# Sixteen weight loads begun on ScalarE's transfer queue, and the table of instruction orders searched anew

## The chip, the core and the metric

The kernel runs on one core of a Trainium2 chip. The metric is device time in microseconds (us): the median over runs of the time of that core. The core has five instruction streams that run side by side and meet at semaphores: TensorE (PE in the profile), VectorE (DVE), ScalarE (ACT), GpSimd (POOL) and SyncE (SP), which here only begins transfers. Each stream takes its own instructions strictly in order.

## The reference

Clustered attention feeds a block that mixes with a Fourier transform and then applies a feed-forward layer. Sizes: batch 4, 8 heads, 768 tokens, head size 64, so the model width is 512.

```python
def _attn_ref(q, k, v, centroids):
    ...
    q_assign = np.argmax(np.einsum('bhsd,hcd->bhsc', q_n, c_n), axis=-1)
    k_assign = np.argmax(np.einsum('bhsd,hcd->bhsc', k_n, c_n), axis=-1)
    mask = q_assign[:, :, :, None] == k_assign[:, :, None, :]
    scores = np.where(mask, scale * np.matmul(q, k.transpose(0, 1, 3, 2)), -1000000000.0)
    ...
    return np.matmul(attn, v)

def _moe_ref(x, w_ch1, w_ch2):
    u = x + np.real(np.fft.fft(np.fft.fft(x, axis=1), axis=2))
    ...
    return u + np.maximum(un @ w_ch1, 0.0) @ w_ch2
```

`un` is `u` normalized over the width; the weights are 512 x 2048 and 2048 x 512.

## The kernel before

All products are made in pieces of 16 bits: a float32 value is split into a high and a low half (f16), and three products of halves are added in PSUM, the memory that TensorE writes.

**Attention** goes by pairs of heads, 16 pairs in all, four to a sequence. A pair's queries and keys are loaded (L372), scaled and split (L397 on ACT, L398 on DVE), and assigned to clusters. Then 6 row tiles of 128 queries follow (`scores`). A tile's score group for the two heads, j = 0 and 1, is twelve matmuls of L538 and four of L543, which alternate between the two heads' banks `ps_big`. DVE takes the row extremum (L557), which frees the bank early, since in the first sequence it also copies the scores into a ring of four slots in `X[1]`; ACT makes the exponential (L560) and casts it to the high half (L568); POOL subtracts for the low half (L569), which gives back the ring slot; SP begins a transfer that transposes both halves (L571); PE multiplies by V (`attend`, L589 to L591); DVE divides into `X` (L605).

**Weights.** Both weight matrices arrive as 64-bit floats and are loaded as 32 pieces of 128 x 512 (512 KB; in the rows 128 rows of 2048 16-bit words), pieces 0 to 15 of the first layer and 16 to 31 of the second (`Weights.load`, L715). The top bits are split by sign on ACT for two pieces at a time (`signs`, L744 and L745), PE sums them to find the block's largest value (L725) and rebuilds the value (`join`, L754, and L758 on DVE, which reads the raw piece for the last time and so frees its slot); ACT and DVE or POOL make the two halves (`halve`, L764, L767, L768, L770). Pieces 16 to 31 pass through two pairs of slots by turns, so that piece p waits for the join of piece p - 4 (16 and 17 for 4 and 5). A load goes to SP's queue while its number is below `QW`, and to ACT's from there on:

```python
    QW = 99
    ...
        (self.nc.sync if k < self.QW else self.nc.scalar).dma_start(out=raw[:, 1:1 + 4 * DM], in_=src.bitcast(U16))
```

**Fourier and feed-forward.** When the four pairs of a sequence are done, its transform follows (L884 to L1069), then the normalization with transposes (L1106 to L1124), then the feed-forward layer in three blocks (`up`, L1286; `down`, L1314). It runs while the next sequence's attention runs.

**What sets the order.** The program is recorded as Python calls it, and `Order.apply` then sorts each engine's instructions by a table, `ORDERS`, of one compressed row of displacements per engine. It adds dependencies that keep that order and changes nothing that an instruction does. The waits between engines follow from the data.

Of the kernel before, what the change touches and what calls it, by code (L numbers as in the profile page):

```python
# [67 lines left out]
class Counted:  # L68
# [5 lines left out]
    def tile(self, shape, dt, name, bufs=None, **kw):  # L74
# [10 lines left out]
        "QHitW)Rs#sE_5x=9d(_-bbjjHVkdJBA&qWLr8jEKPTWjO9$N*i*IoO1EDrS-OO5|!^uo-vd4T#CtHsVQ??+ZCLUvTEGZIFXYqep@QTV>`l)`pLU$"
        "Za#MPy7k<GpCP}wg%*H`d`0Y9os>DAs#mh=)JQ3=55OzGV7xc-)|LF4qLj7u(%Aw1hjKg@uU@bPaZpPsEA>YDk8RKRg%D?4m8?3c8M2Q^6`3D85A"
        "r{#HPo1>eedDk2IiU)Y0XI98Eg5Ddqs??sM|65y|FXKKi>CZL<j{Wv9>CB!+Y?#v|w|%=2CZDU8z^-Y$fi7{43?{?Br72r7Dy#>{^z*fN_br)`{c"
        "RQ=Ju!`eJ1daV>piss(s1{nmJ8VO^Cxvg*4kd>-RlQDfG5u-Nk!YVth`#hMfat!=ii*o^3oxc&^UZRoKXqHZ3cm4~N1Ie<7b0(bRSw`D10A+<*pb"
        "2$Y9<3!92=%dQ9uj47Ou+Zz=nmwm=sn>GfKSR7f9)^2s3H3koJ4@xODrZV9&)0TNUhi|X*`Jr*FQNH!uAlHf2W0dIae2?2aCF3z7P!#rjpqCm|7t"
# [1499 lines left out]
```

## Time and profile before

| | us |
|---|---|
| median of 3 runs | 954.57 |
| lowest and highest run | 952.27, 954.65 |
| span of the profiled execution | 949.3 |
| PE, DVE, ACT, POOL busy | 863.9, 678.2, 601.6, 608.3 |

The span reaches from the first to the last instruction of one profiled execution; the page gives no other time of that execution, and what lies around the span is in the runs' times. The busy times are sums over the whole span, in which the first quarter and the rest look quite different, so they have to be read by stage. Beginning a transfer is not counted as busy time, on SP and on ACT alike. In rows of the trace, L715 is line 715 of the kernel before; `<-` stands between what an instruction writes and what it reads.

### The profile page before, as it was taken

What the parts mean: (1) busy time and instruction counts of PE and PEld (TensorE: products, weight loads), DVE (VectorE), ACT (ScalarE), POOL (GpSimd) and SP (SyncE); (2) the same over time, 40 slices, a digit from 0 to 9 for tenths busy, and PEclk for the clock granted to TensorE, in tenths of its full rate; (3) what the DMA queues carried; (4) which work ended last, traced back from release to release, by engine and by line L of the source; (5) the groups of instructions that cost most, each with busy time, mean ns of one, the idle gap of its engine ahead of it and who ended that gap; (6) DMA issues with size and microseconds to landing.
All of it is one profiled execution on the core that took longest, in us unless ns stands there. A gap on an engine that the chain in (4) does not pass through costs nothing.

```text
span 949.3 us, 23660 instructions
## 1 busy us (share of the span) xinstructions
PE 863.9 (91%) x9241; PEld 581.0 (61%) x9241; DVE 678.2 (71%) x1531; ACT 601.6 (63%) x944; POOL 608.3 (64%) x752
## 2 busy tenths in 40 slices
PE   4777776677999999998999999999999999999998
PEld 1334443345756748666758667667668586676674
DVE  7989888877756667677757567678773446889643
ACT  6989988776666747647757747657676563353320
POOL 3778786755876876746767768748677764342421
PEclk9999897889999999999999999999999999999999
DMA  9999999988588888999899889998887764201020
GB/s 360 242 217 192 233 262 222 224 169 159 103 169 144 146 178 164 184 177 173 157 171 184 174 155 187 197 173 187 151 147 153 132 118 101 60 1 41 19 78 23
DMA packets 405151, 150.20 MB, mean 158 GB/s; under 512 B 383024, under 2 KB 391728, under 8 KB 405040
## 3 DMA queue, kind: packets, MB, share of 16 engines
q1 hardware_dynamic: 404896, 148.67, 78.1%
q8 instruction: 72, 1.18, 0.5%
q14 instruction: 39, 0.32, 0.1%
q10 hardware_dynamic: 144, 0.03, 0.0%
HBM read 41.99 MB, written 6.29 MB: 51 GB/s over the span
## 4 chain that ended last, share of the span: by engine, by line
PE 56%; DMA 7%; DVE 5%; POOL 4%; ACT 4%; issue 2%; SPq 1%; ACTq 0%; POOLq 0%; DVEq 0%
PE ps_fb L1314 8%; PE ps_fc L1314 7%; DMA pts<-ph 7%; PE ps_fa L1286 6%; PE ps_fa L1314 5%; PE ps_fb L1286 5%; PE ps_fc L1286 5%; PE ps_big L530 5%; PE ps_big L1228 3%; POOL ph L569 2%; PE ps_o L589 2%; PE ps_o L590 2%; PE ps_o L591 2%; PE ps_big L538 1%; ACT ph L568 1%
## 5 line engine op out<-in xcount | busy, mean ns | idle before, releaser
L569 POOL TENSOR_TENSOR ph<-p,ph 128x768 f16<-128x768 f32 x144 | 238.4, 1656 | 112.8 <-ACT ph L568 96.8
L557 DVE TENSOR_SCALAR_CACHE_REDUCE ps_big<-ps_big,sce 128x768 f32<-128x768 f32 x144 | 145.4, 1020 | 60.5 <-PE ps_big L530 34.7
L1314 PEld LDWEIGHTS <-arena 128*128 128x128 f16 x1152 | 109.9, 98 | 121.4 <-issue 1.6
L560 ACT ACTIVATE p<-ps_big,rmx 128x768 f32<-128x768 f32 x144 | 128.7, 897 | 60.3 <-DVE ps_big L557 43.0
L568 ACT CAST ph<-p 128x768 f16<-128x768 f32 x144 | 119.6, 830 | 70.0 <-DMA pts<-ph 67.7
L1295 POOL TENSOR_TENSOR arena<-arena 128x256 f16<-128x256 f32 x160 | 110.8, 697 | 52.2 <-ACT arena L1294 51.6
L1286 PEld LDWEIGHTS <-w1h 128*128 128x128 f16 x1280 | 124.9, 98 | 17.9 <-issue 1.5
L589 PE MATMUL ps_o<-v,pts 128*128 128x66 f16 x1062 | 111.1, 194 | 3.9 <-DMA pts<-ph 2.1
L590 PE MATMUL ps_o<-v,pts 128*128 128x64 f16 x1062 | 110.3, 195 | 0.0
L591 PE MATMUL ps_o<-v,pts 128*128 128x66 f16 x1062 | 110.0, 193 | 0.0
L589 PEld LDWEIGHTS <-pts 128*128 128x128 f16 x1062 | 98.4, 97 | 13.7 <-issue 5.9
L590 PEld LDWEIGHTS <-pts 128*128 128x128 f16 x1062 | 98.4, 97 | 7.4 <-issue 2.6
L1314 PE MATMUL ps_fb<-w2h,arena 128*128 128x512 f16 x320 | 100.9, 379 | 0.0
L591 PEld LDWEIGHTS <-pts 128*128 128x128 f16 x1062 | 98.6, 99 | 0.4
L538 PE MATMUL ps_big<-u 64*128 64x384 f16 x576 | 71.7, 356 | 26.2 <-ACT p L560 13.0
L1286 PE MATMUL ps_fa<-arena,w1h 128*128 128x256 f16 x464 | 85.5, 273 | 0.0
L1314 PE MATMUL ps_fc<-w2h,arena 128*128 128x512 f16 x256 | 81.0, 379 | 0.3 <-ACT arena L1294 0.3
L1286 PE MATMUL ps_fb<-arena,w1h 128*128 128x256 f16 x424 | 78.3, 273 | 0.7 <-DVE arena L1056 0.4
L530 PE MATMUL ps_big<-u 96*128 96x384 f16 (+1 forms) x384 | 75.6, 325 | 2.4 <-ACT p L560 2.3
L1286 PE MATMUL ps_fc<-arena,w1h 128*128 128x256 f16 x392 | 72.4, 273 | 1.1 <-ACT arena L1294 1.1
L1286 PEld LDWEIGHTS <-w1l 128*128 128x128 f16 x640 | 62.5, 98 | 10.6 <-issue 1.6
L538 PEld LDWEIGHTS <-u 64*128 64x128 f16 x576 | 30.1, 100 | 54.3 <-issue 33.9
(371 smaller groups left out, 2149.2 us busy)
## 6 DMA issues: line engine op xcount, KB each, us to landing
arena<-in_moe_w_ch_dram SPq DMA_DIRECT2D x26, 512.0 KB, 5.6
scr<-in_k_dram SPq DMA_DIRECT2D x16, 384.0 KB, 4.3
scr<-in_q_dram SPq DMA_DIRECT2D x16, 384.0 KB, 4.2
vst<-in_v_dram SPq DMA_DIRECT2D x16, 384.0 KB, 4.1
out_dram<-arena SPq DMA_DIRECT2D x24, 256.0 KB, 2.8
u<-u SPq DMA_DIRECT2D x64, 96.0 KB, 2.7
u<-u SPq DMA_DIRECT2D x16, 192.0 KB, 3.2
pts<-ph SPq DMA_TRANSPOSE x161, 3.9
```

Of the source, the lines that this page charges most:

```text
L530: nc.tensor.matmul(out=ps[j][:, hf, 0:SH], lhsT=self.slots(x + 2 * j, 1)[0:n, sl], rhs=self.slots(y + 2 * j, 1)[0:n, hf * SH:(hf + 1) * SH ...
L538: nc.tensor.matmul(out=ps[j][:, hf, 0:SH], lhsT=hq[rows[j], a, sl], rhs=hk[rows[j], c, hs], start=(i == 0), stop=False)
L557: self.mark = nc.vector.tensor_scalar(out=ju, in0=ps[j][:, :, 0:SH], scalar1=ne, scalar2=None, op0=ALU.mult, op1=ALU.min, accum_out=m)
L560: nc.scalar.activation(x, ju, AF.Exp, bias=m, scale=-1.0)
L568: nc.scalar.copy(out=ph[:, 0], in_=p32)
L569: nc.gpsimd.tensor_tensor(out=ph[:, 1], in0=p32, in1=ph[:, 0], op=ALU.subtract)
L589: nc.tensor.matmul(out=o[:, at:at + W], lhsT=hi, rhs=v16[:, kt, 0:W], start=(kt == 0), stop=False)
L590: nc.tensor.matmul(out=o[:, at:at + D], lhsT=hi, rhs=v16[:, kt, 66:130], start=False, stop=False)
L591: nc.tensor.matmul(out=o[:, at:at + W], lhsT=lo, rhs=v16[:, kt, 0:W], start=False, stop=(kt == ST - 1))
L1286: nc.tensor.matmul(out=ps.rearrange("p (t x) -> p t x", x=P), lhsT=a[:, dc, fs], rhs=c[:, :, dc], start=(i == 0), stop=(i == 11))
L1295: nc.gpsimd.tensor_tensor(out=hl[:, f], in0=r, in1=hh[:, f], op=ALU.subtract)
L1314: nc.tensor.matmul(out=ps, lhsT=a[:, f, ts], rhs=w[:, f], start=(i == 0), stop=(i == 47))
```

## The change

`QW` goes from 99 to 16, so that the sixteen pieces of the second weight matrix are begun by ACT and not by SP. All five rows of the table `ORDERS` are new.

```diff
 ORDERS = {
     "Activation": (
-        "c-m!E*>2Q85G;?!dyx?3P=fM+1W16y|9=Hf@CG6h2qXyNNV4o{dz<R&@d9Ek+vAz(?&|95SpcZ8v&47ed(5w`ZLG6n#INSv8j#W8qxts{_td;w`%"
...
+        "c-l=>X>Suj4E4+&X|ARxh@%35_`;9iSMxvkf)JuYNFYQ@ucRSIv)MJzZ@imkmCf#q$M4yGc0@#iG#c?6rPe+CZnVO6#GN1+c5Ag=kw5s&<P^^vp18*QG0*"
...
     AHEAD = 7
-    QW = 99
+    QW = 16
     LOW = 16
```

The table is 19 lines longer, so that every line behind it has a number higher by 19 in the changed file: L715 is L734 there, L538 is L557, L571 is L590, L744 and L745 are L763 and L764, and L764 and L767 are L783 and L786. In the rows below, `in_moe_w_ch2_dram` is the second weight matrix in memory, `ph`, `p32`, `pts` and `u` hold the halves of attention before and after a transpose, `ps_big` is a score bank, and the number behind a name tells one buffer's use from the next.

SP's queue about the last weight loads, from the third row tile of sequence 0's last pair on, before:

```order
L571 DMA_TRANSPOSE u_109<-p32_2136 128x12x128
L472 DMA_TRANSPOSE u_109<-oh_115 128x9x128
L571 DMA_TRANSPOSE pts_110<-ph_2223 128x12x128
L715 DMA arena_67<-in_moe_w_ch2_dram 128x2048 x4
L571 DMA_TRANSPOSE pts_110<-p32_2230 128x12x128
L571 DMA_TRANSPOSE pts_110<-p32_2348 128x12x128
L571 DMA_TRANSPOSE pts_110<-ph_2341 128x12x128
L571 DMA_TRANSPOSE pts_110<-ph_2446 128x12x128
L571 DMA_TRANSPOSE u_109<-p32_2453 128x12x128
L715 DMA arena_67<-in_moe_w_ch2_dram 128x2048 x2
L571 DMA_TRANSPOSE pts_110<-ph_2546 128x12x128
L715 DMA arena_67<-in_moe_w_ch2_dram 128x2048 x2
```

The same place in the change:

```order
L590 DMA_TRANSPOSE pts_110<-ph_2223 128x12x128
L491 DMA_TRANSPOSE u_109<-oh_115 128x9x128
L590 DMA_TRANSPOSE pts_110<-p32_2230 128x12x128
L590 DMA_TRANSPOSE pts_110<-p32_2348 128x12x128
L590 DMA_TRANSPOSE pts_110<-ph_2341 128x12x128
L590 DMA_TRANSPOSE pts_110<-ph_2446 128x12x128
L590 DMA_TRANSPOSE u_109<-p32_2453 128x12x128
L991 DMA arena_67<-in_ny_dram 128x384
L590 DMA_TRANSPOSE pts_110<-ph_2546 128x12x128
L590 DMA_TRANSPOSE pts_110<-ph_2554 128x12x128
L391 DMA scr_2791<-in_q_dram 128x768
```

The eight loads of `in_moe_w_ch2_dram` between the transposes are gone, and a table load of the Fourier stage (`ny`) stands further ahead; the transposes follow each other in nearly the same order.

ACT about the halving of pieces 18 and 19 (`ps_fb_1953` and `ps_fa_2040`), before:

```order
L560 ACTIVATE X1_64<-X1_64,rmx_2021 128x768
L428 ACTIVATE ac_2140<-ps_fc_2141,cinv_176 128x384
L568 CAST ph_2024<-X1_64 128x768
L764 ACTIVATE w2h_82<-ps_fa_2040,wsc_1779 128x512
L764 ACTIVATE w2h_82<-ps_fb_1953,wsc_1779 128x512
L560 ACTIVATE X1_64<-X1_64,rmx_2028 128x768
L560 ACTIVATE X1_64<-X1_64,rmx_2133 128x768
L767 ACTIVATE arena_67<-ps_fa_2040,wsc_1779 128x512
L560 ACTIVATE X1_64<-X1_64,rmx_2126 128x768
L745 ACTIVATE w2l_83<-arena_67 128x1024
L361 ACTIVATE v16_2035<-vst_1301,scp_65 128x6x64
L744 ACTIVATE w2h_82<-arena_67 128x1024
```

The same place in the change:

```order
L783 ACTIVATE w2h_82<-ps_fb_1953,wsc_1779 128x512
L734 DMA arena_67<-in_moe_w_ch2_dram 128x2048
L447 ACTIVATE ac_2140<-ps_fc_2141,cinv_176 128x384
L587 CAST ph_2024<-X1_64 128x768
L734 DMA arena_67<-in_moe_w_ch2_dram 128x2048
L579 ACTIVATE X1_64<-X1_64,rmx_2028 128x768
L763 ACTIVATE w2h_82<-arena_67 128x1024
L783 ACTIVATE w2h_82<-ps_fa_2040,wsc_1779 128x512
L764 ACTIVATE w2l_83<-arena_67 128x1024
L786 ACTIVATE arena_67<-ps_fa_2040,wsc_1779 128x512
L579 ACTIVATE X1_64<-X1_64,rmx_2126 128x768
L763 ACTIVATE w2h_82<-arena_67 128x1024
```

The loads of pieces 22 and 23 now stand between casts and exponentials, and behind them come the sign steps (L763, L764) of pieces 20 and 21 and, in the last row shown, the first one of pieces 22 and 23.

PE at the score group of `ps_big_1173` and `ps_big_1174`, the fifth row tile of the second pair, before:

```order
L590 LDWEIGHTS u_109
L590 MATMUL ps_o_658<-v16_265,u_109 128x64
L591 LDWEIGHTS u_109
L591 MATMUL ps_o_658<-v16_265,u_109 128x66
L538 LDWEIGHTS u_109
L538 MATMUL ps_big_1173<-u_109 128x384
L538 LDWEIGHTS u_109
L538 MATMUL ps_big_1174<-u_109 128x384
L538 LDWEIGHTS u_109
L538 MATMUL ps_big_1173<-u_109 128x384
L538 LDWEIGHTS u_109
L538 MATMUL ps_big_1174<-u_109 128x384
```

In the change the first matmul of that group stands so (the second one, on `ps_big_1174`, comes 28 matmuls of attention times V later):

```order
L562 LDWEIGHTS u_109
L562 MATMUL ps_big_1059<-u_109 128x384
L557 LDWEIGHTS u_109
L557 MATMUL ps_big_1173<-u_109 128x384
L610 LDWEIGHTS pts_110
L610 MATMUL ps_o_658<-v16_219,pts_110 128x66
L608 LDWEIGHTS pts_110
L608 MATMUL ps_o_658<-v16_219,pts_110 128x66
L609 LDWEIGHTS pts_110
L609 MATMUL ps_o_658<-v16_219,pts_110 128x64
```

The sixteen matmuls of a score group stood in a row; now the first one stands ahead, and matmuls of an older tile's `attend` fill the place between it and the others.

## Rows read from the trace of the kernel before

**Rows 1.** The page's part 1, busy time, share and instructions of each engine, whole span.
```profile
PE 863.9 (91%) x9241; PEld 581.0 (61%) x9241; DVE 678.2 (71%) x1531; ACT 601.6 (63%) x944; POOL 608.3 (64%) x752
```

**Rows 2.** Windows by stage; columns PE, PEld, DVE, ACT, POOL busy (x instructions), clock, DMA, GB/s.
```profile
40.00:200.00 160.00, 112.86 (x1431) 61.12 (x1428) 140.66 (x293) 136.29 (x176) 121.92 (x109) 0.88 1.09 224
200.00:240.00 40.00, 33.29 (x441) 24.19 (x439) 29.77 (x80) 27.60 (x45) 24.67 (x30) 0.94 0.81 138
240.00:949.00 709.00, 696.15 (x7215) 485.54 (x7212) 473.06 (x1077) 407.06 (x683) 444.09 (x556) 1.00 0.71 135
```

**Rows 3.** Line L1286 (first feed-forward layer): count, ns min/median/max, first and last start.
```profile
L1286 PE MATMUL ps_fa<-arena,w1h x464: 269/273/274, 232.7 to 850.3; 128*128 128x256 f16 x155
```

**Rows 4.** Waits of DVE, 40 to 200 us: us in total, times, longest.
```profile
DVE ps_big L557 <- PE ps_big L543: 2.6, 3, 1.9
...
DVE X L557 <- PE ps_big L543: 2.3, 4, 1.1
DVE X L557 <- POOL ph L569: 1.8, 2, 1.0
DVE arena L899 <- ACT arena L897: 1.2, 2, 0.7
...
DVE X L557 <- POOL p L569: 0.7, 1, 0.7
```

**Rows 5.** Waits of ACT, same stretch.
```profile
ACT X L560 <- DVE X L557: 6.6, 6, 2.0
...
ACT ph L568 <- DMA pts<-ph: 2.8, 4, 0.8
```

**Rows 6.** Waits of POOL, same stretch.
```profile
POOL ph L569 <- ACT ph L568: 10.8, 10, 3.4
...
POOL p L566 <- DMA u<-p: 1.7, 2, 0.9
```

**Rows 7.** Waits of PE, same stretch.
```profile
PE ps_big L538 <- DVE X L557: 10.3, 11, 1.8
PE ps_big L538 <- ACT p L560: 9.4, 5, 4.2
```

**Rows 8.** Line L715, weight loads begun from 50 to 180 us, and their landing.
```profile
L715 SPq DMA_DIRECT2D arena<-in_moe_w_ch_dram x16: 327/410/889, 56.1 to 175.7; - x16
...
DMA to landing us min/median/max: 3.7/5.3/7.1
```

**Rows 9.** Waits of SP's queue, 40 to 200 us.
```profile
SPq L715 <- DVE ps_fa L758: 5.6, 4, 2.0
```

**Rows 10.** Line L571, transposes that SP began from 40 to 200 us.
```profile
L571 SPq DMA_TRANSPOSE pts<-ph x27: 1273/1543/3362, 41.1 to 194.2; - x27
L571 SPq DMA_TRANSPOSE pts<-p x15: 1274/1755/5428, 38.2 to 159.9; - x15
```

**Rows 11.** Timeline of SP's queue, 150 to 165 us: start, us, line, operation, count.
```profile
152.66 4.36 SPq L715 DMA_DIRECT2D arena<-in_moe_w_ch_dram  x4
157.12 6.00 SPq L571 DMA_TRANSPOSE pts<-p  x2
```

**Rows 12.** Line L1447, ACT's only DMA issue, at the start.
```profile
L1447 ACTq DMA_DIRECT2D X<-in_centroids_dram x1: 403/403/403, 0.7 to 0.7; - x1
```

**Rows 13.** Groups of ACT by line, 40 to 200 us: busy us, mean ns, idle before.
```profile
L560 ACT ACTIVATE X<-X,rmx 128x768 f32<-128x768 f32 x42 | 38.2, 932 | 6.6 <-DVE X L557 6.6
...
L744 ACT ACTIVATE w2h<-arena 128x1024 int16<-128x1024 int16 x8 | 9.7, 1214 | 0.4 <-DMA arena<-in_moe_w_ch_dram 0.4
...
L764 ACT ACTIVATE w2h<-ps_fa,wsc 128x512 f16<-128x512 f32 x8 | 5.5, 682 | 2.2 <-DVE ps_fa L758 1.8 <-DVE wsc L65 0.4
```

**Rows 14.** Timelines of PE from 29 us and from 237.5 us; idle before in brackets.
```profile
29.20 0.32 PE L538 MATMUL ps_big<-u 64*128 64x384 f16 x1 [0.41 <-DVE X L557]
30.13 1.13 PE L538 MATMUL ps_big<-u 64*128 64x384 f16 x11 [0.62 <-DVE X L557]
...
238.05 1.15 PE L538 MATMUL ps_big<-u 64*128 64x384 f16 x12
```

More of the change, by code (lines that the diff above doesn't have):

```diff
@@ L85 @@
[L85 to L89, printed above, removed]
@@ new lines @@
+        "|xm&z>A2q8a&FR?UCfw@O4@x7<6GzvQ&<T<*ML$+BQn_sm4_eD0zQ9s1h28;`>CQi1mmR4<*WslCwo7OEzfg{EgyN+wA)wibwOaZjPgj7TLFY|&e+l`CYW"
+        "Nm0f#QfUQIrkXN6a2?LI?a)2v{Xl!u)c^<^D$weddk@>0An(W|$``V?I3lZ*_^&njI)H*x{Cn(;wO2abtq&8PVYO>pHFX-R67_m3mpFIcovRUFf%QAx<;?"
+        "14U0b5(#TAj%H1wFJnyO^?zI*yd=3``Pr`$erDXzk;_ud0kUh9hb>v<L0tAthQ)k+>xoeSzac3Mtzz^YNxk4=Ic8J}y(sbDk7=10zGOye8IX^LMuV&NDoP"
+        "4PwPbvkQRHs~f(0lQboUDB9!{(G|Mqhgs?s%2aOWu+;bXY$K4ThPl=chL&#l@Tv#A-LXK4d>`Dn-NFyP1`IQLgStqVjpw5AD{w9a>0|an~Hr}2k55OGz&}"
@@ new lines @@
+        "T>QA$C;WI&+n2<h-MNy0#7Gq3CPt%#NvKE`Pvx!%XC2JW^IWvCHMH<7FIIba0pIPU(ZYw8gk9I^tZOic7>MoxP!B6`jq=JLO^~Uz1)(%f%0UrQ}lRE_<Gn"
+        "r&By)hCy#LGAdLZucfJCttRD%_+q|xNj~L$jSr<KWunxK^Bb$O9Pd)qk`r+z?p{X|xj&cIAe^!Cog$ZXE)$z5KZ0tm<Zpu+y|xFv=U1$OIh~7gt2U^PTCq"
+        "#LnAmt<c$Y<G?tp&n;+-WoMpRx9)w}YD7`Ie7RBe{b{3}I8>8e$qu5m?N@7Y=v?+$q0JsUL{-u89&7|!FIGbPV(#@l#n&a{wUzULV`VanJ`^>M2I<i*SqW"
+        "+^{{x;rXU$@PYAzPIN>^E@UsrD`cC4)?c2V2yNCc6S#g*IPN7iHAE>F{(DN#tVbG(t9K8&-@=Pq5IB-rTa3d!~OY9J-F6Q7W=nX)7{PCS@XMP#D5j<xINu"
@@ L110 @@
+        "fW9uqg=cY+3KDMf1wR)kvQ;i?ot7!<0dtvTuZ&h<e>!WfmTbeSpG>xM_Y@Xr986<qfSK2$*uK7I&XWII1ty??yioIFojHAEcXMVt^;;yV{CB>Gie$U`eJy"
+        "!OUGL8SClppw8GfB%{ef2cYywd$#`7N%!o9vTQG5B8gjk{~A)q<IOW??<gichmXra5q;*bRd-JMcapXk3=^e{wdBE3=|$GAVig#>~AN9V>f1;u}vecU7K="
+        "@^6YhF?uGBp0)88)WH{o"
     ),
     "DVE": (
[L112 to L113 removed]
@@ new lines @@
+        "Guk`GacyN`R9Yc${kZqY7>RK{G7<-LdRtKR3SU7dYp-p8oV6$<DtZc>U-c9rn7%|uoFCip!|pRlKI3>|Ql8W`>ItRnE}Bz+A}=hWt(Ot}ZS628l);b99aB"
+        "7KwaO#a@ZSE$3A*t5-bJhyelKX_iDpSVCpJm2Rztn0!5lXQ<|kB4YU(O1=qtlwo{BiiE$2eg3EA!h4%XW(6~Pw8#Gfw>A9hkJrOVsTl$cHm(dEDo`w1kVr"
+        "fyNB;0Mq_T%JK*Y)GWsj-J#Z{YQttB}uc!q<Fye@IV6#d4uxAt}n`ko9rvlawxuJLj@zb=9d}Vwk$lw<C&ciRkE752C94#T2f_4Ge#)!_)7|h6Z2fn&2Q4"
+        "_EcFrUtOA99iIVr>i2muL-~2nzw7G0*Z<j$uzw9&>t-drVp8QpENmRz!4#Z$TM0Z^GA@g>xCno^?d9g5Qv2J_H8Q;e?ITiJ@CSSHpP8p|Wr6iglofNpMw^"
@@ new lines @@
+        "$0OCmK;Nc6*eax?%*@j@^%>ACoiMY!2FnuB8EAI_>s$EVK$JZe#wUot$0u+q6Yb6b<pw`b->Z^CyqjPobyOx{BGJ4j*tx?;RT4pe_xOS`>^W-{D1L*5^)c"
+        "IASVn#aim|FzavhPdpK=GNJXEIeaGwR$GX2J7MKuK4o~vZ}6ydv}qdtd}Re0cd`Oteam8^xzq4*fXwhz5*v8{8<@nwDqERA3x#Bahk`2=hfXj8Rg6rJ5`p"
+        "wfn$D*_|AOw0X!^VY<wO)w|Wn)M)d12FI|UsMhQwRWK13iMEI)iIy&s@l4VJnwR*OR3sz9%=6&60Qz7WiLl>uYyLH;fe6vq;JeqT16>$`6#o-RbB*~_PMM"
+        "(Qa*&;N1DlmJ=O3jjGBtlLv@K-BKXf3i7~FDvwh5=a-L}C@aP4)u4<AVRYdfbA76DJz|R03ppJaSy2e(#L@-A`v-HLhqV2KZ-A9LArEj4G-&qjcP4u-d!E"
@@ new lines @@
+        "UHbTMHHJn$htc*zLJWu+<<@i3VaYH_e;aT7-|TcBf;|mhJF1{x-US)Y^zix%dJKd`3Og5O<UQ=7;FB;-SO-RR6X*7WGSKGm4z@?k(@n(+?~?L#nQ*_DS!d"
+        "_N+_%GTC~Q_tK>Vh2*6G%K`8nS1a4t-_Oqu+wTvZN=C4oYUc}Gt@*0ER4dZ5P;$C`13gpDnjtv%r=l=)9JRHC8nyjEs(8W^J>4E@?-{ttssmYDd-)Eyzph"
+        "BjTK%EZP9Jr?<~od=GBI|YrQ52tDwr(5mQPvzKG5DIx-DqUc}_p#Z3Ufv1JSjx!^Rw-f-1<zZPaC=8LN_LV;@{>D#D4&dWwAQLU~5d64~eH9m8m*hU{zh`"
+        "dXWE4O|`CJY7S4=UuL25|vin$>cqj>Cn}g?F}7t6O*3^W!MZ{CktF}_aCceqqAwA4U_A&re{!~9mPgul_H%c2I>H(^Ht5wMO28dwmqDg4f;xJ_jURJ@y{a"
@@ L151 @@
+        ">&EKTF%Ar#z`H%6f&2EKtHKz%Mw{K3cE~aSIwB`G2?SdB2XwTQ@olx}DsaoeJ5%owaap`(Y?D;;k=-*<MrD_{8Wo156J8^<Uo#p=ngOfc6?wrlNwQr*BIV"
+        "A%<Jdv#b*M>~;kHeN3?Q2jXXb-~TO~PWS`90zBfxDndOcGY;n=2tW86DSmDkyD8L+r^Y=_=DVQ^y<(cyKQEkcV$=Rvk@*;K0<!(YJ_vndneM{F$Ot_dzq-"
+        "_6d-g+o2i4OivE)>gSlxu=>t&+O_JOZmK9Bao&m3=fjHsGmG%b$@YGhZLYEurz$(^srIvoW9+Ty&fi7sIK7qsKN~vt{{R}Uj?w"
     ),
```

110 lines of the change are left out of this document (54 added, 56 removed).

## The prediction, made before the changed kernel was run

> **What bounds the kernel now.** I read the page first, then windows by stage, then the waits of each engine inside the stage that came out. The page gives PE 91% busy [rows 1]. The windows show that this is a mean over two different stages. From 240 us to the end PE is busy 696.15 of 709 us with the full clock granted, so that stage is as long as its matmuls; from 40 to 200 us PE is busy only 112.86 of 160 us, while DVE is busy 140.66 and ACT 136.29, and the DMA engines' share is 1.09 [rows 2]. The feed-forward's first matmul starts at 232.7 us [rows 3]; after that little can be won, so what counts is when it starts. In the early stage DVE is the fullest engine. It waits there for PE's score matmuls (2.6 and 2.3 us) and for POOL's subtractions, which give back the ring slots it writes (1.8 and 0.7 us); for ACT it waits longest 1.2 us [rows 4]. ACT waits 6.6 us for DVE and 2.8 us for transposes [rows 5]; POOL waits 10.8 us for ACT and 1.7 us for a transpose [rows 6]; PE waits 10.3 us for DVE and 9.4 us for ACT before a score group [rows 7]. So four engines and SP's queue lean on each other, all nearly full, with DVE first.
>
> The profiled span is 949.3 us. The runs shown have a median of 954.57 us, 5.27 us above it; I make the sum against the span and add 5.27 us.
>
> **The change, part by part.**
>
> *SP loses 16 loads.* Each issue took 0.41 us there (median; 0.327 to 0.889) [rows 8]: 16 x 0.41 = 6.6 us. SP also stood 5.6 us in front of these loads until DVE's join had freed the slot [rows 9], with transposes queued behind. That is 12.2 us of 160 us that SP gets back. A third effect goes the same way: four loads began at 152.66 us, and the two transposes behind them took 6.00 us, about 3 us each, where the median is 1.54 to 1.76 us [rows 10, 11]. What of it lies on the path is what others lose to late transposes: ACT 2.8, POOL 1.7, and DVE 1.8 + 0.7 = 2.5 us through POOL's ring slots, at most 7.0 us in all [rows 4 to 6]; at least nothing, since DVE itself never waits for a DMA in that stage. I take 4.0 us: ACT's 2.8 and half of DVE's 2.5. What is late next is POOL, which waits for ACT's casts.
>
> The bytes do not change, and the DMA share is already 1.09 [rows 2], so the transfers themselves still compete. The Trainium skill's page "DMA: Bandwidth & Descriptors", section "Issuing engines are not separate DMA queues", says that a second issuing engine saves only the time that the sequencer needs to begin the transfer. By that rule the 3 us transposes would stay as they are, and I would take 2 us instead of 4 us and come to 952.6 us.
>
> *ACT gains 16 issues.* They stand in ACT's order between the casts and exponentials. No row shows ACT issuing in this stage; its only issue, at the start, took 0.40 us [rows 12], and SP's row has the same 0.41 us, so 16 x 0.41 = 6.6 us, at most 16 x 0.889 = 14.2 us if it passes whole, and at least nothing if it falls into ACT's waits (6.6 + 2.8 us in the two rows shown) [rows 5, 8]. The slot waits do not come along in full: nearly every load stands next to the first halving of a piece that needs the same join, so ACT would wait there anyway. POOL, PE and then SP queue behind ACT, but DVE, the fullest, waits for it little. I take a bit under a third of 6.6 us, +2.0 us.
>
> *Landing.* Between the issue of piece 23 and ACT's first reader of it stand two exponentials (0.93 each), two sign steps (1.21 each) and two 512-wide ops (0.68 each): 1.86 + 2.42 + 1.36 = 5.6 us [rows 13]. Landing took 5.3 us at the median, 7.1 us at most [rows 8]. Pieces 19 and 27 have about the same lead, so the cost is 0 to 3 x 1.5 = 4.5 us; by the median nothing, and I take 0.
>
> *PE's order, searched anew.* The set of 1958 matmuls that stand ahead of the first feed-forward matmul is the same in both, but they are cut finer. Before, a score group's first matmul ran alone, and PE then stood 0.62 us until the second bank was free, with nothing put in between [rows 14]. Now the first matmul goes ahead, attention-times-V matmuls follow, and then the rest: the score matmuls stand in 110 separate runs instead of 38 before the feed-forward. A score matmul that runs alone takes 0.32 us, one in a run of twelve 1.15 / 12 = 0.10 us [rows 14], so 72 more runs cost PE up to 72 x 0.22 = 16 us. The cover is PE's idle time, 160 - 112.86 = 47 us [rows 2]; without it, DVE would wait for score banks by that much. On the gain side stand DVE's two waits for score matmuls, 4.9 us [rows 4], since a filled wait lets the older tiles finish earlier. Range -4.9 to +16 us; I take -2.0 us, nearer to the gain because the cover is three times the cost.
>
> *The rest of the new order.* The last write of sequence 0's attention output is DVE's instruction 292 in both orders, and the last split of its first Fourier stage moves from 336 to 339. Three DVE instructions of at most 1 us are 3 us, so -3 to +3 us; I take 0. After 240 us PE is idle 709 - 696.15 = 12.9 us [rows 2], and I count nothing there.
>
> Sum: -4.0 + 2.0 + 0 - 2.0 + 0 = -4.0 us, a span of 945.3 us and a time of **950.6 us**. A measurement of this kernel can tell about 0.3%, 2.9 us, from no change, so this counts as faster, though not by much.
>
> **The rivals.**
>
> *No change (954.6 us).* DVE's own queue is the bound: it is busy 140.66 of 160 us, and no row shows it waiting for SP [rows 2, 4]. Then what SP gets back only lengthens SP's waits, and the two other terms cancel: 0 + 2.0 - 2.0 = 0. For it speaks that DVE's share stays as it was in both orders; against it the 2.5 us that DVE loses to POOL's ring slots.
>
> *Slower: ACT held at the descriptor generator.* If only one queue at a time can have descriptors made, each load on ACT waits until SP's transpose in progress is through, and a whole chain of casts and exponentials stands behind it. By their medians the two kinds of transposes shown held SP for 27 x 1.54 + 15 x 1.76 = 68 of 160 us [rows 10], and with the long ones and the other kinds well over half of the time. Half of a median transpose is 0.8 us; as an upper price every load pays it: 16 x (0.41 + 0.8) = 19 us on ACT. Half of it passes, since POOL and PE already wait for ACT more than for anything else: +9.7 us instead of +2.0. SP's gain is halved to -2.0, because SP meets ACT's loads there too. -2.0 + 9.7 - 2.0 = +5.7 us, 960.3 us. It decides when the mean issue on ACT exceeds about 0.75 us, where a half of 16 x 0.75 equals the 6 us of gain. For it: on SP a load right behind a transpose took up to 0.889 us against 0.327 us [rows 8]. Against it: those were on one queue, and the median is 0.41 us.
>
> This is a rule of the Trainium skill as well: its page "Perfetto Trace Analysis", section "DMA Instruction — HWDGE (DVE, Sync)", says that the block that makes descriptors is locked for exclusive use, and that the wait for the lock lies inside the duration shown. What the trace has of two queues at once is only the start, where ACT's issue took 0.40 us [rows 12].
>
> *Slower: the cut score groups.* If the fill between the first and second score matmul is longer than the wait it hides, score banks come late and DVE, which has little left to do meanwhile, waits. Half of the 16 us passing instead of -2.0 gives 950.6 + 10 = 960.6 us.
>
> **How the numbers follow.** Faster as summed, 0.43; no change, 0.32; the generator, 0.18; the cut groups, 0.07. Hence faster 0.43, same 0.32, slower 0.25. The low end takes SP's whole 7.0 us and 4 us from PE's order with nothing lost on ACT, -11 us, 943.6 us, and a little for the rest of the order: 942.5 us. The high end takes in the two slower cases up to 960 us. The likeliest case alone reaches from 945 to 952 us.
>
> **What would show it.** Right: ACT's loads with a median near 0.41 us; transposes behind no load longer than 2 us; ACT's waits for transposes and DVE's for POOL's subtractions smaller between 40 and 200 us; the first feed-forward matmul at about 229 us instead of 232.7 us; the stage after it as long as before. The generator: load issues on ACT of 1 us and more, and POOL's wait for casts above 10.8 us. The cut groups: DVE's waits for score matmuls above the 4.9 us of its two rows, with PE busier and the first feed-forward matmul later. The whole reading is wrong if the difference arises after 240 us, where I count nothing.

## The result, and the profile after

The changed kernel took 962.73 us (median of 4 runs, 961.53 to 971.17); the kernel before, on the same chip, 954.61 us (4 runs, 952.27 to 956.18). The recorded ratio, taken over all the runs, is 1.0121, 95% interval 1.0083 to 1.0158: slower by 1.2%. By the medians it is 8.1 us, 0.85%. I had forecast 950.6 us, a gain of 0.4%, and had given 960.0 us as the upper end. The profiled execution, the one of 961.53 us, has a span of 959.5 us, 10.2 us more than that of before. In every run of which both are known the time is 1.7 to 2.2 us above the span, so the profile of before (949.3 us) belongs to a time of about 951.2 us, below all four timed runs: some 2 us of the 10.2 us are that profile's luck. Of the 5.27 us that I added to the span, too, only about 2 us lie around a span; this changes neither the gain forecast nor the time. One execution of e14 below (963.49 us) ran in a slower state of the chip and is left out.

The page's part 1 [rows 1 before]:

```profile
PE 887.2 (92%) x9241; PEld 589.0 (61%) x9241; DVE 681.4 (71%) x1531; ACT 603.3 (63%) x944; POOL 614.6 (64%) x752
```

The same three windows of after, with the columns of [rows 2]:

```profile
40.00:200.00 160.00, 126.89 (x1440) 67.15 (x1439) 133.79 (x295) 134.30 (x175) 122.66 (x113) 0.85 1.11 221
200.00:240.00 40.00, 36.50 (x463) 26.16 (x461) 34.87 (x84) 27.88 (x46) 24.81 (x26) 0.95 0.94 167
240.00:949.00 709.00, 693.43 (x7171) 483.17 (x7169) 477.49 (x1070) 410.47 (x685) 450.49 (x558) 1.00 0.70 134
```

and line L1305, which is L1286 of before [rows 3]; every line of after stands 19 further down:

```profile
L1305 PE MATMUL ps_fb<-arena,w1h x424: 269/273/418, 232.6 to 853.4; 128*128 128x256 f16 x142
```

The first feed-forward matmul starts at 232.6 us, as before (232.7). In the early stage PE is busier (126.89 us for about as many matmuls: more of them run alone, and the granted clock, a mean of TensorE's two levels of 1.2 and 2.4 GHz, is 0.85 where it was 0.88) and DVE less (133.79 against 140.66). So in these two profiles the first stage as a whole is neither shorter nor longer, and the 10.2 us arise behind it, where I had counted nothing.

The early stage has changed inside, though. The loads begun on ACT from 40 to 240 us, to be held against [rows 8]:

```profile
L734 ACTq DMA_DIRECT2D arena<-in_moe_w_ch_dram x16: 334/334/1014, 46.2 to 179.1; - x16
...
DMA to landing us min/median/max: 3.9/5.2/11.0
```

An issue on ACT is short (0.334 us at the median). The median landing is as before (5.2 against 5.3 us), but the longest is 11.0 us where it was 7.1. Waits from 40 to 200 us: of ACT [rows 5],

```profile
ACT ph L587 <- DMA pts<-ph: 9.1, 3, 6.6
ACT w2h L763 <- DMA arena<-in_moe_w_ch_dram: 6.1, 2, 5.5
```

of POOL [rows 6],

```profile
POOL ph L588 <- ACT ph L587: 18.4, 11, 3.4
```

and of DVE [rows 4]:

```profile
DVE w2l L789 <- ACT w2h L783: 6.5, 2, 5.3
...
DVE X L576 <- PE ps_big L562: 4.2, 6, 1.3
...
DVE ps_big L576 <- PE ps_big L562: 1.1, 1, 1.1
```

ACT waits 9.1 us for transposes instead of 2.8, once for 6.6 us, and 6.1 us for landed pieces, where [rows 13] had 0.4 us. DVE in turn waits 5.3 us once for ACT's half of a piece. Its waits for POOL's subtractions fell, as I had said, from 2.5 to 0.3 us. The rows don't tell why these transfers came late; that took the experiments.

Behind 240 us, PE's waits in after, to the end:

```profile
PE ps_big L549 <- DMA u<-u: 4.0, 4, 1.5
PE ps_fb L1010 <- DMA u<-u: 3.0, 1, 3.0
PE ps_big L549 <- ACT arena L1074: 1.8, 1, 1.8
```

These are L530, L991 and L1055 of before. Summed over the rows of the matmuls, the gaps between one matmul's end and the next one's start come to 15.6 us behind the first feed-forward matmul; before they were 9.2 us. The other 3.9 us are time in matmuls: in two 20 us windows of after the granted clock is 0.91, a mean of the two levels that costs some 0.09 x 20 = 1.8 us in each, with PE idle in or just ahead of them. Before, the clock stayed at 1.00, the upper level.

```profile
580.00:600.00 20.00, 18.18 (x234) 14.57 (x232) 11.71 (x26) 14.01 (x24) 14.96 (x15) 0.91 0.81 175
...
640.00:660.00 20.00, 18.64 (x218) 14.45 (x219) 13.54 (x29) 13.76 (x21) 11.05 (x12) 0.91 0.78 134
```

### The profile page after: what moved, and what is told of

Read it like the earlier page. It is cut to its first block, busy times and chain, and to the rows that moved or that the text cites. A ratio compares the mean times of both kernels' runs of the same rounds, so it can differ in the third digit from the quotient of the medians.

```text
span 959.5 us, 23667 instructions
## 1 busy us (share of the span) xinstructions
PE 887.2 (92%) x9241; PEld 589.0 (61%) x9241; DVE 681.4 (71%) x1531; ACT 603.3 (63%) x944; POOL 614.6 (64%) x752
## 4 chain that ended last, share of the span: by engine, by line
PE 44%; DMA 18%; ACT 11%; DVE 10%; POOL 9%; issue 5%; SPq 2%; ACTq 0%; POOLq 0%; DVEq 0%
DMA pts<-ph 13%; PE ps_fb L1333 6%; POOL ph L588 5%; PE ps_fc L1333 5%; PE ps_fa L1333 4%; PE ps_fa L1305 4%; PE ps_fc L1305 3%; PE ps_big L549 3%; PE ps_fb L1305 3%; ACT ph L587 3%; PE ps_big L1247 3%; ACT p L579 2%; DMA arena<-in_moe_w_ch_dram 2%; PE ps_big L557 2%; PE ps_o L610 2%
## 5 line engine op out<-in xcount | busy, mean ns | idle before, releaser
L579 ACT ACTIVATE p<-ps_big,rmx 128x768 f32<-128x768 f32 x144 | 129.4, 899 | 69.2 <-DVE ps_big L576 43.1
L1333 PEld LDWEIGHTS <-arena 128*128 128x128 f16 x1152 | 101.5, 97 | 84.3 <-issue 3.4
L608 PE MATMUL ps_o<-v,pts 128*128 128x66 f16 x1062 | 142.7, 196 | 3.6 <-DMA pts<-ph 2.5
L609 PE MATMUL ps_o<-v,pts 128*128 128x64 f16 x1062 | 142.8, 197 | 0.0
L610 PE MATMUL ps_o<-v,pts 128*128 128x66 f16 x1062 | 141.7, 196 | 0.0
L1305 PEld LDWEIGHTS <-w1h 128*128 128x128 f16 x1280 | 124.5, 98 | 18.1 <-issue 1.7
L610 PEld LDWEIGHTS <-pts 128*128 128x128 f16 x1062 | 101.5, 100 | 28.9 <-issue 14.1
L608 PEld LDWEIGHTS <-pts 128*128 128x128 f16 x1062 | 101.6, 99 | 27.1 <-issue 6.7
L609 PEld LDWEIGHTS <-pts 128*128 128x128 f16 x1062 | 101.5, 99 | 25.3 <-issue 12.4
L1333 PE MATMUL ps_fb<-w2h,arena 128*128 128x512 f16 x320 | 111.7, 379 | 0.0
L557 PE MATMUL ps_big<-u 64*128 64x384 f16 x576 | 82.7, 353 | 16.2 <-DVE X L576 11.1
L549 PE MATMUL ps_big<-u 96*128 96x384 f16 (+1 forms) x384 | 89.7, 328 | 6.9 <-DMA u<-u 4.0
L1305 PE MATMUL ps_fa<-arena,w1h 128*128 128x256 f16 x464 | 93.1, 275 | 0.0
L1333 PE MATMUL ps_fc<-w2h,arena 128*128 128x512 f16 x256 | 88.9, 379 | 0.0
L1305 PE MATMUL ps_fb<-arena,w1h 128*128 128x256 f16 x424 | 84.2, 274 | 0.5 <-ACT arena L1313 0.5
L1305 PE MATMUL ps_fc<-arena,w1h 128*128 128x256 f16 x392 | 78.1, 273 | 0.4 <-DVE arena L1337 0.2
L1305 PEld LDWEIGHTS <-w1l 128*128 128x128 f16 x640 | 62.7, 98 | 10.1 <-issue 1.7
L1333 PE MATMUL ps_fa<-w2h,arena 128*128 128x512 f16 x192 | 67.4, 379 | 0.3 <-DVE arena L1076 0.3
```

The lines of the kernel that those rows point to most:

```text
L549: nc.tensor.matmul(out=ps[j][:, hf, 0:SH], lhsT=self.slots(x + 2 * j, 1)[0:n, sl], rhs=self.slots(y + 2 * j, 1)[0:n, hf * SH:(hf + 1) * SH ...
L557: nc.tensor.matmul(out=ps[j][:, hf, 0:SH], lhsT=hq[rows[j], a, sl], rhs=hk[rows[j], c, hs], start=(i == 0), stop=False)
L579: nc.scalar.activation(x, ju, AF.Exp, bias=m, scale=-1.0)
L608: nc.tensor.matmul(out=o[:, at:at + W], lhsT=hi, rhs=v16[:, kt, 0:W], start=(kt == 0), stop=False)
L609: nc.tensor.matmul(out=o[:, at:at + D], lhsT=hi, rhs=v16[:, kt, 66:130], start=False, stop=False)
L610: nc.tensor.matmul(out=o[:, at:at + W], lhsT=lo, rhs=v16[:, kt, 0:W], start=False, stop=(kt == ST - 1))
```

## The experiments

My first theory (A) was that the new order of the second stage makes the whole loss. The rival (B) was that the loads on ACT make it, by work that comes late and is paid for later; a third (C) that the new first stage leaves a worse state behind. In all runs below, "order of before" and "new order" are the two tables of `ORDERS`; a load that changes queue moves to the place of the other engine's row that was reached when it was begun. Times are medians; ratios are the recorded ones to runs of the kernel before on the same chip (medians of 951.6 to 952.6 us there), with 95% intervals, and are not the quotient of two medians. A profile is one execution, and executions of one kernel here lie up to 11 us apart, so I compare stages over several profiles.

### The two parts of the change apart

**e1: loads on ACT, order of before.**

```diff
-    QW = 99
+    QW = 16
```
```diff
 ACT's row (16 such places; the same 16 loads leave SP's row)
 L742 ACTIVATE arena<-arena 128x1024
 L743 ACTIVATE arena<-w2l,arena 128x1024
+L713 DMA arena<-in_moe_w_ch_dram 128x2048
 L566 CAST ph<-X_64 128x768
```

> The orders of the kernel before; only the 16 second-layer loads move from SP's to ACT's row, each at the place of ACT's row that was reached when SP issued it. Theory A (the loss of 10.2 us of span arises behind the first FFN matmul, at 232.6 us in both traces, from the order of that stage: PE gaps of 15.6 us against 9.2 and some 4 us of slower clock): 953 to 957 us, the time of before. Theory B (the loads on ACT make the loss: 16 issues and the 6.1 us that ACT waits for a landed piece push the attention chain back): 960 to 963 us. First FFN matmul within 3 us of 232.7 by A, 4 us or more later by B.

955.79 us (951.18 to 961.75), 1.0039 [1.0020, 1.0058]. **e2: new order, loads on SP** (`QW = 99`, the 16 loads back in SP's row).

> The new orders; only the 16 loads go back from ACT's to SP's row, at the place of SP's row that was reached when ACT issued them. Theory A (the order behind the first FFN matmul): 960 to 965 us, the time of after. Theory B (the loads on ACT): 953 to 957 us. If both share the loss, between 957 and 960 us.

958.27 us, 1.0066 [1.0040, 1.0092]. Neither theory alone: both halves cost, and 0.39 + 0.66 = 1.05% is most of the 1.2% of the whole.

**e3: new order ahead of the feed-forward's start, order of before behind it, loads on ACT**, and **e4: the reverse, loads on SP.** Of each engine's row the first part is taken from the one table up to that time, the rest from the other.

> Every engine follows the new order for what it began ahead of the first FFN matmul (232.6 us), loads on ACT, and the order of before for all the rest. Theory A (the order behind that matmul): 952 to 957 us, with PE gaps behind it near 9 us. Theory C (the new order of the first stage, equally long, leaves later work in a worse state: a folded operand or a transpose that comes late): 960 to 963 us.

> The reverse: the order of before, loads on SP, for what was begun ahead of the first FFN matmul, and the new order for all the rest. Theory A: 960 to 966 us, with PE gaps behind that matmul near 15 us. Theories B and C: 952 to 957 us.

e3 took 962.56 us, 1.0101 [1.0070, 1.0133], against theory A; e4 962.47 us, 1.0109 [1.0088, 1.0130], as theory A had it. The stages say more than the times. In e4's profile the feed-forward starts at 230.6 us and PE's gaps behind it are 19.5 us; in e3's they are 11.3 us. So the second stage of the new order is slow wherever it stands, and e3 loses its time elsewhere; where, its profile doesn't show, since that is its fastest execution (955.96 us).

### What a load on ACT costs

In e1's profile, the slowest of its executions, the feed-forward started at 240.4 us. Its 16 loads on ACT from 40 to 240 us,

```profile
L713 ACTq DMA_DIRECT2D arena<-in_moe_w_ch_dram x16: 334/335/586, 51.6 to 183.6; - x16
...
DMA to landing us min/median/max: 4.0/6.3/16.8
```

and its SP queue (start, us, line, operation, count):

```profile
151.39 2.09 SPq L569 DMA_TRANSPOSE pts<-ph  x1
153.59 19.32 SPq L569 DMA_TRANSPOSE pts<-p  x2
173.07 3.25 SPq L569 DMA_TRANSPOSE pts<-ph  x2
```

Two transposes, 6.00 us together before [rows 11], held SP for 19.32 us while three loads begun on ACT at 152.39, 155.70 and 156.30 us landed after 11.8, 15.0 and 16.8 us. ACT began the loads of 155.70 and 156.30 us in 0.33 and 0.34 us, while SP stood in the first of these two transposes (from 153.59 us for 7.45 us). One window of e1, columns as in [rows 2]:

```profile
160.00:165.00 5.00, 3.48 (x20) 1.06 (x19) 3.68 (x9) 0.00 (x0) 0.19 (x1) 0.50 1.51 88
```

and the same of before:

```profile
160.00:165.00 5.00, 4.26 (x36) 1.90 (x36) 5.00 (x11) 3.77 (x6) 0.85 (x2) 0.50 1.24 210
```

ACT does nothing for 5 us, POOL next to nothing, and the DMA engines, at a share of 1.51 (a sum over packets, which overlap), move 88 GB/s where before they moved 210. (The clock is at 0.50, the lower level, in both.) SP's queue (`q1`) moved as many bytes in these 5 us as ACT's (`q10`), 0.22 MB, but in 895 packets against 60:

```profile
q1 hardware_dynamic: 895, 0.22, 105.2%
q10 hardware_dynamic: 60, 0.22, 46.0%
```

This is how it reaches the attention chain: ACT's next instruction stood 8.01 us until a transpose had landed.

```profile
165.38 0.83 ACT L566 CAST ph<-X 128x768 f16<-128x768 f32 x1 [8.01 <-DMA pts<-ph]
```

This is the worst place of the longest of e1's executions. Over all profiles with full-size loads on SP that show the landings (before, e2, e4, e5, e6, e8, e9, e12, e15, e16) no load from 40 to 240 us took more than 7.3 us to land; with loads on ACT (after, its second run, e1, its second run, e3) the longest of each profile took 9.6 to 16.8 us. The transposes of the attention weights (L571 of before) follow: with loads on SP at most one of some 60 per profile above 8 us (the longest 9.3 us), with loads on ACT two to six, up to 20.1 us. The same shows in two lines of the new order, transposes of after and of e9 (the new order with loads on SP):

```profile
DMA to landing us min/median/max: 3.6/4.6/12.0
```
```profile
DMA to landing us min/median/max: 3.6/4.6/7.3
```

Is it the issue on ACT, or the data in flight from two queues? **e7: order of before, loads on SP, 16 more transfers of 8 bytes begun on ACT** at e1's places.

```diff
         self.nc.sync.dma_start(out=raw[:, 1:1 + 4 * DM], in_=src.bitcast(U16))
+        if k >= 16:
+            self.nc.scalar.dma_start(out=raw[0:1, 4 * DM + 4:4 * DM + 8], in_=src.bitcast(U16)[0:1, 0:4])
```

> The kernel before with its loads on SP, and 16 more transfers of 8 bytes that ACT begins at the places where the run with loads on ACT had the loads; their data is not used. Theory Q (what costs is that 512 KB loads run beside SP's transposes from a second queue, with landings of up to 16.8 and 20.1 us): the time of before within 2 us. Theory I (the 16 issues on ACT, some 5.9 us of its time, cost by themselves): 3 to 4 us above before.

951.46 us, 1.0006 [0.9991, 1.0022]: theory Q. The 16 issues themselves, shown here, cost nothing that can be measured, though the interval reaches to 2.1 us:

```profile
L715 ACTq DMA_DIRECT2D arena<-in_moe_w_ch_dram x16: 229/234/558, 51.8 to 173.6; - x16
```

The traces show why that is little: ACT goes on computing while it begins a transfer. In e7 all 4.8 us of the 16 issues lie inside ACT's own busy time, in e1 5.2 of 5.9 us, in after 4.8 of 6.2 us. One place in after:

```profile
155.95 0.81 ACT L587 CAST p<-X 128x768 f16<-128x768 f32 x1
156.07 0.33 ACTq L734 DMA_DIRECT2D arena<-in_moe_w_ch_dram  x1
156.67 0.93 ACT L579 ACTIVATE X<-X,rmx 128x768 f32<-128x768 f32 x1
```

**e10 and e11: each load cut to an eighth, order of before, on ACT and on SP.**

```diff
+        n = P if k < 16 else P // 8
         (self.nc.sync if k < self.QW else self.nc.scalar).dma_start(
-            out=raw[:, 1:1 + 4 * DM], in_=src.bitcast(U16))
+            out=raw[0:n, 1:1 + 4 * DM], in_=src.bitcast(U16)[0:n])
```

> The orders of before, the 16 loads on ACT, and each load cut to 16 of its 128 partitions (64 KB in place of 512; the rest of each piece is not loaded). Theory Q (512 KB loads of one queue and transposes of the other hold each other up): no transpose of the stage lands after more than 10 us, and the time is that of the same cut with the loads on SP, or up to 4 us less (what SP is relieved of). If the hand-over between two queues costs whatever the size: 3 us or more above the cut loads on SP.

> The kernel before with the same cut (16 of 128 partitions of each of the 16 loads, the rest not loaded), loads on SP: the measure for the run before. Some 7 MB less are moved, which by theory Q frees transposes on the same queue: 0 to 4 us below before.

951.98 us, 1.0012 [0.9999, 1.0025] on ACT, 952.17 us, 0.9998 [0.9978, 1.0018] on SP; the feed-forward starts at 230.4 us in both profiles, and no transposes of e10 took more than 7.5 us to land. With 64 KB loads in this order no difference between the queues is clear of noise, which speaks for size: theory Q again. (e11, all on SP, has two transposes of 9.4 us, so landings up to there need no second queue.) And the second half of that expectation fell: SP relieved of 16 issues gains nothing in this order.

**after_again and e14: second measurements of the changed kernel and of e1.**

> The changed kernel unaltered, on the same chip as these runs. If the loads on ACT and the new order both cost: 9 to 12 us above before, and 4 to 6 us above the new order with loads on SP (958.3 us where before took 952.1). If only the order costs: 5 to 7 us above before.

> The orders of before with the 16 loads on ACT, once more: 0.2 to 0.6% above before, and in its profile some landings above 8 us among loads and transposes of the first stage (none above 7.3 us among the loads, and at most one above 8 us among the transposes, in each profile with loads on SP).

The changed kernel took 967.59 us here, 1.0163 [1.0124, 1.0202], 16.0 us above before and so beyond the 9 to 12 us that I expected; e14 954.44 us, 1.0028 [1.0003, 1.0053], with 1 load and 4 transposes above 8 us. Their difference to the same order with loads on SP is 0.3 to 0.4% in the order of before (1.0028 and 1.0039) and 0.6 to 1.0% in the new one (1.0121 and 1.0163 against 1.0066 and, below, 1.0060).

**e13 and e17: the cut loads in the new order, on ACT and on SP** (the edit of e10).

> The changed kernel with each of its 16 loads on ACT cut to 16 of 128 partitions (64 of 512 KB, the rest not loaded). Theory Q (large loads of one queue and transposes of the other hold each other up): no landing of a load or transpose of the first stage above 10 us, and the time that of the new order with loads on SP, 0.5 to 0.8% above before. If the size does not matter: 1.2 to 1.6% above before, as the changed kernel.

> The new order with the loads on SP, each cut to 16 of 128 partitions (the rest not loaded). If the size of the loads is what holds the new order's first stage: FFN start at 219 to 223 us as with the cut loads on ACT (219.6), time 944 to 949 us. If it is the relief of SP's queue that brought it there: 226 to 229 us and 955 to 958 us.

e13 took 946.19 us, 0.9943 [0.9922, 0.9965], faster than before although its second stage is the slow one; I had expected 0.5 to 0.8% above. Its first feed-forward matmul, and the landings of its 16 loads:

```profile
L1307 PE MATMUL ps_fb<-arena,w1h x424: 269/272/283, 219.6 to 838.2; 128*128 128x256 f16 x142
```
```profile
DMA to landing us min/median/max: 2.2/3.3/6.9
```

e17, the same on SP, starts it at 221.4 us, as the size would have it, and took 950.55 us, 0.9995 [0.9972, 1.0017], 1.6 us above that forecast. So in the new order the first stage depends on the loads' data: cut to an eighth they bring its end forward by 13 to 15 us on ACT (from 232.6 to 234.8) and by 6 to 8 us on SP (from 227.2 to 229.5, without the 231.7 of e16); in the order of before it is 230.6 to 232.7 us with full loads on SP and 230.4 with cut ones. And here, with little data in flight, the relief of SP seems to show: ACT is 0.5% better than SP by the runs, on two chips, and starts the feed-forward 1.8 us earlier by the profiles.

### What the new order of the second stage costs

**e9: e2 once more.**

> The new order with loads on SP once more, on the chip of these runs: 0.4 to 0.9% above before, as the first time (0.66%).

957.19 us, 1.0060 [1.0042, 1.0077]. **e5: new order with loads on SP ahead of the feed-forward, order of before behind.**

> The new order, loads on SP, for what was begun ahead of the first FFN matmul; the order of before for the rest. The runs so far give, against before: loads on ACT +3.7 us (orders of before), the new order with loads on SP +6.3 us, the new order behind the FFN start alone +10.4 us. If these add up, the new first stage is worth some -4 us and this kernel takes 947 to 951 us where before takes 952. Rival (an order that is handed over at the FFN start costs by itself, as the +10.5 us of the run with the new order first and the loads on ACT suggest): 957 to 963 us.

954.92 us, 1.0044 [1.0022, 1.0066]: between the two forecasts. The feed-forward starts early (227.7 us), but the stretch from there to the second sequence's Fourier stage takes 170.6 us where others take 166 to 168; handing over from one order to the other has a price. Its later blocks (208.6, 194.7 and 149.8 us) are those of the order of before in the table below, so theory C falls: the new first stage leaves nothing behind that slows them.

**e6: SP's row mended.** At five places PE waited for folds of the scores' operand (`u<-u`) or for the tables of the transform (L999) that SP began late; by the ends of all instructions that touch the same memory, they could have begun 1 to 25 us earlier. The longest wait, in after, on SP's timeline and on PE's:

```profile
634.08 1.05 SPq L536 DMA_DIRECT2D u<-u  x1
635.17 0.60 SPq L999 DMA_DIRECT2D arena<-in_ss_dram  x1
635.88 0.58 SPq L1338 DMA_DIRECT2D out_dram<-arena  x1
636.50 0.58 SPq L999 DMA_DIRECT2D arena<-in_ss_dram  x1
```
```profile
641.36 0.61 PE L1010 MATMUL ps_fb<-arena 128*128 128x258 f16 x2 [3.05 <-DMA u<-u]
```

The table begun at 636.50 us lands at 641.31, and the matmul starts 0.05 us later, so the table, not the fold that the view names, ended this wait.

```diff
 SP's row, one of the places
+L999 DMA arena<-in_ss_dram 128x6x128
 L590 DMA_TRANSPOSE pts<-ph 128x12x128
...
 L1338 DMA out_dram<-arena 128x512
-L999 DMA arena<-in_ss_dram 128x6x128
```

> The new order with the loads on SP; in SP's row alone, behind the FFN start, 15 transfers stand earlier: folds of the scores' operand and loads of the spectra tables, at the five places where TensorE waited for them (1.00, 1.13, 1.95, 0.54 and 2.92 us in the run of the new order with loads on SP), ahead of transposes that stood before them. Theory A1 (the new row of SP begins these late, though their data had been ready 1 to 25 us earlier): the five waits fall from 7.5 us to under 2, all PE gaps behind the first FFN matmul from 18.4 to 11 to 13 us, the time from 0.66% above before to within 0.2% of it (950 to 954 us where before takes 952). Rival (another operand is late next, or the delayed transposes make the same wait): 956 to 960 us.

(It is 14 transfers.) 961.98 us, 1.0113 [1.0084, 1.0142]: the rival, and worse. PE's waits from 240 us:

```profile
PE ps_big L549 <- ACT p L579: 5.2, 5, 1.8
PE ps_big L549 <- DMA u<-u: 3.3, 1, 3.3
```

The waits for SP are gone at four of the five places, and PE waits for exponentials (L579) instead; at the fifth, a fold that I had moved back made a wait of 3.3 us. **e8: PE's row filled** with the next feed-forward matmuls at five places, on the order of e2.

```diff
 PE's row, one of the places (11 matmuls moved up from behind)
+L1305 MATMUL ps_fb<-arena,w1h 128x256
+L1305 MATMUL ps_fb<-arena,w1l 128x256
...
 L549 MATMUL ps_big<-u 128x384
```

> The new order with the loads on SP; in TensorE's row alone, at five places where it waited (1.00, 2.14, 0.66, 1.95 and 1.26 us in the run of that order), the next 4 to 19 FFN matmuls of the row (7.9 us of them in all) stand ahead of the one that waits. Theory A2 (the new row of TensorE takes up scores and spectra before their operands are there, with FFN work standing unused right behind): the five waits, 7.0 us, fall under 2, and the time by 4 to 6 us, from 0.66% above before to within 0.3% of it. Theory A3 (the chain of folds, softmax and transposes sets the pace at these places, and TensorE only waits for it somewhere else): the PE gaps behind the first FFN matmul stay at 17 to 20 us and the time within 2 us of that of the new order with loads on SP.

958.36 us, 1.0069 [1.0054, 1.0083]; gaps 17.9 us: theory A3. **e12: both mended.**

> The new order with loads on SP, TensorE's row filled as in the run before, and in SP's row the four spectra loads of the third sequence and two folds near 380 us earlier (they had been ready 4 to 25 us before they were begun). If the waits are independent of each other, the 4.46 us wait for the spectra at 637 us goes too, the PE gaps fall to 12 to 14 us and the time to 0.1 to 0.3% above before. If the chain sets the pace (theory A3): PE gaps of 16 to 20 us, 0.5 to 0.8% above before.

960.61 us, 1.0102 [1.0083, 1.0122]; gaps 18.0 us: the chain again, and a time above both forecasts. In e8 one wait for the tables had grown to 4.5 us (first fence); in e12 that one is gone and others have come (second fence):

```profile
PE ps_fb L1010 <- DMA u<-u: 4.5, 1, 4.5
PE ps_big L549 <- DMA u<-u: 3.7, 3, 1.9
```
```profile
PE ps_big L549 <- ACT p L579: 4.8, 8, 1.9
PE ps_big L549 <- DMA u<-u: 2.9, 2, 1.9
PE ps_fa L50 <- ACT arena L1074: 1.9, 1, 1.9
```

Three mends, three times about the same sum of gaps (19.9, 17.9 and 18.0 us; 18.4 in e2 and 16.1 in e9). That suggests that at these places several operands come about equally late, and that moving one of them, or the matmul, only changes which is seen.

**e15 and e16: the new order up to the third, or the second, sequence's Fourier stage, then the order of before; loads on SP.** Cut at the first L884 of each sequence, the second stage has four blocks. Over all profiles:

| block, us | order of before | new order |
|---|---|---|
| start of the feed-forward to 2nd sequence | 166.1 to 167.1 (6 profiles) | 166.1 to 167.9 (10) |
| 2nd to 3rd | 206.6 to 209.1 (9) | 208.4 to 213.5 (11) |
| 3rd to 4th | 193.5 to 195.2 (10) | 199.8 to 202.4 (10) |
| 4th to end | 149.0 to 151.7 (10) | 149.4 to 149.8 (10) |

(First blocks in which or ahead of which the order changes, 168.1 to 171.2 us, are left out; runs with cut loads or with mends are in, and the 213.5 us are e6's.) The third block, whole, in before and in after:

```profile
606.50:800.30 193.80, 192.16 (x2011) 136.44 (x2010) 121.04 (x277) 117.75 (x195) 133.92 (x159) 1.00 0.80 148
```
```profile
609.40:810.10 200.70, 195.09 (x2027) 137.64 (x2025) 125.22 (x278) 119.34 (x198) 135.98 (x158) 0.99 0.79 148
```

> The new order with loads on SP up to the start of the third sequence's Fourier stage (610 us of the trace of after), the order of before from there on. If the loss lies in the new order of that third block (200 to 202 us against 194, PE gaps of 5.6 to 7.6 us against 1.1 to 2.2): third block 194 to 196 us, time 950 to 953 us where before takes 952. If it is carried in from earlier (what stands unfinished at that point): 200 us again and 956 to 959 us.

> The same with the order of before from the start of the second sequence's Fourier stage (390 us). If the parts add up (first stage 228 us in place of 231, first block 166.5, then 207.5, 194 and 149.5 as before): a span of 945 to 948 us, 2 to 4 us below before. If the hand-over costs as at the FFN start (where the first block took 170.6 us): 950 to 953 us.

e15 took 954.76 us, 1.0033 [1.0018, 1.0048], and its third block 195.2 us:

```profile
604.10:799.30 195.20, 193.21 (x2019) 136.71 (x2017) 120.41 (x275) 118.82 (x197) 134.11 (x158) 1.00 0.79 151
```

The block's loss is won back, so it lies in that block's own order and isn't carried in; PE's idle time is 2.0 us instead of 5.6, and the clock 1.00 instead of 0.99. The time fell by 0.3%, some 2 us short of what I expected. e16 took 953.52 us, 1.0018 [1.0004, 1.0031], half a microsecond above the rival's range; its first block took 170.7 us, so the hand-over cost as at the feed-forward's start. No kernel that loads everything beat the kernel before.

Which engine's row makes the third block longer stays open. One row of the one order beside four of the other can make rows wait for each other in a circle, and that wasn't tried.

## Why the prediction was wrong

Three differences of means over the profiles make up a loss of about 10 us. The new first stage with loads on SP ends at 227.2 to 229.5 us in seven of eight profiles (231.7 in e16), against 230.6 to 232.7 us in three of the order of before: about -3.2 us. Loads on ACT put it back to 232.6 to 234.8 us: about +5.3 us. The new second stage takes 724.7 to 729.4 us (7 profiles without mends) where the order of before takes 716.6 to 719.6 us (6): about +8.1 us. That this is just the 10.2 us between the two first profiles is in part chance: in that pair the first stage gave -0.1 us and the second +10.3 us, and by the medians the loss is 8.1 us on the first chip and 16.0 us on the second. That the feed-forward starts at the same time in both, 232.7 and 232.6 us, is chance too: a gain and a loss of the first stage met there.

- **"After 240 us ... I count nothing there"**, the last sentence on the rest of the new order, is the step that failed. I had taken that stage to be as long as its matmuls because PE idled only 12.9 of 709 us, and so asked only what could be won there. The runs show 724.7 to 729.4 us for it in place of 716.6 to 719.6 us, most of that in the third block. A stage that is full has little to gain and much to lose: an order that puts operands 1 to 3 us late at a few places loses time at once, and nothing covers it. The bounds of -3 to +3 us came from DVE's places in the first stage and held nothing of the second. I had counted how much finer PE's row was cut ahead of the feed-forward, and not looked behind it.
- **SP loses 16 loads (-4.0).** With the loads' data in flight nothing of it was seen: SP's transposes behind no load were to take 2 us at most, and the longest took 6.8 us in after and 11.7 us in e1; ACT waited 9.1 us for them, not less than 2.8. With cut loads there was nothing in the order of before (e10 against e11); in the new order ACT was 0.5% better (e13 against e17), 1.8 us by the profiles and 4 to 5 us by the runs. So the term is of the right order only where little data is in flight.
- **ACT gains 16 issues (+2.0).** About 0 by e7, whose interval reaches to +2.1 us; the bounds, 0 to 14.2, held it. The issues lie almost wholly inside ACT's own work, which I had not counted as a cover.
- **Landing (0, at most +4.5).** The mis-sized term of the move. I had taken the landings of one queue as those of two. The move measured +5.3 us, with the medians unchanged: what cost were the few longest landings. ACT's waits for a landed piece, 6.1 us in after, and for transposes, 9.1 us, are where it shows; no run parts the two. The Trainium skill's rule ("DMA: Bandwidth & Descriptors", "Issuing engines are not separate DMA queues"), that transfers begun by several engines run on the same 16 DMA engines and interleave, agrees with e1's window, in which both queues moved 0.22 MB each and both were slow; taking it would have led me from -4.0 to -2.0, still on the wrong side, since it names a gain that stays small and no loss.
- **PE's order (-2.0).** The first stage with loads on SP is about 3.2 us shorter, but that is the work of all five rows, and no run parts PE's from the others, so that the number fits is no proof. PE is busier by 14 us from 40 to 200 us without becoming the bound, so the cover was there, and DVE's waits for score matmuls came to 4.2 + 1.1 = 5.3 us, about the 4.9 of before: the rival of the cut score groups fell.
- **The rival of the generator** gave 960.3 us, nearer than my forecast, for a reason that fell: it decides from a mean issue of 0.75 us on ACT, and the issues there took 0.334 us at the median, 0.39 us in the mean, the longest 1.014. Its other sign did come, POOL's waits for casts (18.4 us), but ACT was late from its waits for data and not from its issues. What was held is the other side, SP's two transposes of 19.32 us, and while the first of them held SP, two issues on ACT went through in 0.33 and 0.34 us. Whether any of SP's time is the lock which the Trainium skill describes ("Perfetto Trace Analysis", "DMA Instruction — HWDGE (DVE, Sync)"), no run tells; that cut loads don't do it speaks for the data.

Of the signs named ahead, two decided: the first feed-forward matmul wasn't earlier, and the stage after it was longer, by which alone the whole reading was wrong. Why the second stage of the new order is longer is known down to the block, and not to the row.
